# The end of an attention pipeline written as an order of its own, with two more buffers for expert weights

## The chip, the cores and the metric

The kernel runs on one core of a Trainium2 chip. The metric is the device time of one execution in microseconds (us). The kernel before took 780.9 us, the median of three runs (780.63 to 781.72).

## What is computed

Three stages follow each other. Attention has 4 x 8 heads of 576 tokens and 64 features, and keeps of each row the 32 largest scores. A soft mixture of experts (8 experts with 4 slots each) works on its output, and an MLP with a piecewise quadratic activation on that.

```python
scores = scale * np.matmul(q, k.transpose(0, 1, 3, 2))
kth = np.partition(scores, -32, axis=-1)[..., -32:-31]
scores = np.where(scores >= kth, scores, -1e9)
attn = softmax(scores)                    # over the keys
x = (attn @ v), heads side by side        # 2304 x 512
logits = x @ phi                          # 2304 x 32
d = softmax(logits, axis=0)               # over all tokens: what goes into a slot
slot_input = d.T @ x
slot_out[e] = np.maximum(slot_input[e] @ w1[e], 0) @ w2[e]
c = softmax(logits, axis=1)               # over the slots: back to the tokens
x = c @ slot_out
h = x @ w_in
g = where(h >= 1, h, where(h <= -1, 0, (h + 1) ** 2 / 4))
out = g @ w_out
```

## The kernel before

Attention works on 16 pairs of heads. A pair has five row blocks: blocks 0 to 3 have 128 query rows for each of two heads, block 4 the last 64 rows of both. Each block goes through some twenty steps, named by one letter, then row block and half: `S` scores on PE, `C` copies them to SBUF on ACT, `G` and `L` find the 24 largest on DVE, `M` masks what is among them (on POOL or DVE), `O` counts the mask on ACT, `X` makes the scores again on PE with the kept ones pushed far down by a product with the mask, `Y` takes the next eight by MAX8, `K` and `B` (POOL) make thresholds, `P` (ACT) and `U` (POOL) push down what is below them, `E` takes the exponential on ACT, `T` turns the row on PE into `pt_ps`, `Q` and `R` copy the turned row on ACT, `A` multiplies it with v on PE, `H` takes the result from PSUM on ACT. Blocks 3 and 4 of every pair go "by product": in place of `O` and `X`, a product on POOL (`V`, L418, tile `w`) takes the 24 largest out, and `M` is on DVE and counts as it masks.

`ORDER` is a list of these steps with a lag of 0 to 4 pairs. The loop at the end of the attention runs over frames; in frame f a step with lag k works on pair f - k. This is the order in which PE, ACT, DVE and POOL get their instructions (`manual_schedule`), and each takes them in that order. The last frames are the same list with the steps left out that have no pair any more. What follows the loop, `moe_last` (L671), was not in such an order: a planner placed its instructions.

In the last pair, blocks 3 and 4 take a shortcut (`last_pair`, L777): the exponential of the raw row (`ex`, L789) and the mask by threshold in one step on DVE (L791) in place of `P`, `U`, `E`. Its bias `nm` is made by POOL just before. Each row block of the last pair divides by its sum (`H`, L528), is turned once more (`xT_ps`) and copied to `xT`. `pt_ps` is one buffer of one PSUM bank.

`moe_last` then makes the logits of the last four pairs (`moe_ps`, L683) in three pieces of 256, 256 and 64 tokens; of each piece it takes the maximum, the exponential, turns it, multiplies it with x (`weigh`, L662) and adds it to `acc`. When `acc` is complete it is turned (`si_ps`) and copied to `siT`, which the first product of the experts (`ex_in`, L952) reads.

Expert weights are 64 tiles of 512 KB; the list `worder` says in which order SP loads them. `wload` takes the next free slot from `wfree`: tiles of their own first, then buffers of the attention that are used no more. Buffers of q and k, `ssb`, and four half-slot pairs (`xu` with `v_sb`, two of three `mb`, four `ptb`) come free in the drain, the four last ones after the loop (L823). After 36 tiles come two of w_out, then memory of the attention's pools.

Of the kernel before, what the change touches and what calls it, by code (L numbers as in the profile page):

```python
# [7 lines left out]
ET = mybir.EngineType  # L8
# [66 lines left out]
'''.split()  # L75
GA = 3
# [4 lines left out]
def kernel_body(tc, qT, kT, vP, phi, w1, w2, w_in, w_out, out, fast, flag):  # L81
# [35 lines left out]
    worder[36:36] = [(4, 0, f) for f in range(SOON)]  # L117
# [77 lines left out]
    n_x = sum(width) - n_v  # L195
    cnt_all = p_moe.tile([P, NPAIR * n_x], F32, name="cnt_all")
    less_all = p_moe.tile([P, NPAIR * n_v], F32, name="less_all")
    kn_all = p_moe.tile([P, NPAIR * n_v, 2], F32, name="kn_all")
# [82 lines left out]

    def at(u, j):
        of_v = u[1] in BY_V
        before = sum(width[r] for r in range(u[1]) if (r in BY_V) == of_v)
        return u[0] * (n_v if of_v else n_x) + before + j
# [84 lines left out]
    def op_m(u, j):  # L370
# [6 lines left out]
        if u[1] in BY_V:  # L377
# [42 lines left out]
    def op_y(u, j):  # L420
        if not fast:
            return
        if u[1] in BY_V:
# [34 lines left out]

    def op_t(u, j):
# [51 lines left out]
    def op_h(u):  # L511
# [9 lines left out]
        if r == 0:  # L521
            x_of[pi] = (p_xh.tile([P, 9, D], F32, name="xh", tag="xh"), p_xT.tile([P, S], F32, name="xT", tag="xT"))
        xh = x_of[pi][0]
        rd = p_small.tile([P, 2], F32, name="rd", tag="rd")
        nc.vector.tensor_scalar_add(rd[:, :n], av[:, :n, D], 1e-9)
        nc.vector.reciprocal(rd[:, :n], rd[:, :n])
        for j in range(n):
            nc.scalar.activation(xh[:, 2 * r + j, :], av[:, j, :D], AF.Copy, scale=rd[:, j:j + 1])  # L528
        emit_xT(pi, [r])
# [20 lines left out]
    def xT_flip(pi, rows):  # L550
        xh = x_of[pi][0]
        ps = ps_m.tile([P, NR, P], F32, name="xT_ps", tag="m_ps")
# [34 lines left out]
    def moe_quarters(b):  # L587
# [38 lines left out]
        nm = p_moe.tile([P, 1], F32, name="nmn", tag="nmn", bufs=3)  # L626
# [39 lines left out]
    def join_quarters():  # L666
        ps = ps_m.tile([P, P], F32, name="rq_ps", tag="m_ps")
        nc.tensor.matmul(ps[:, :1], same.rearrange("p r s -> p (r s)"), run_q, start=True, stop=True)
        nc.vector.tensor_copy(run_s, ps[:, :1])

    def moe_last(b, pieces, pool):  # L671
        def bank():
            nbank[0] += 1
            return pool.tile([P, 512], F32, name="moe_ps", tag=("s_ps", "x_ps", "pt_ps")[nbank[0] % 3], bufs=1)

        xs = [x_of[b * NHP + hp] for hp in range(NHP)]
        c0, c1 = pieces[0][0], pieces[-1][1]
        main = [r for r in range(NR) if c0 <= r * P < c1]
        mid = c1 == S
        for a, z in pieces:  # L680
            ps = bank()
            for c in range(NHP):
                nc.tensor.matmul(ps[:, :z - a], phi_sb[:, c].rearrange("p g s -> p (g s)"), xs[c][1][:, a:z],  # L683
                                 start=(c == 0), stop=(c == NHP - 1))
            yield
            nc.scalar.copy(lT[:, a:z], ps[:, :z - a])
            yield
        own = slice(b * NSLOT, (b + 1) * NSLOT)
        nc.vector.tensor_copy(lall[own, c0:c1], lT[own, c0:c1])
        mb = p_moe.tile([P, 1], F32, name="mb", tag="mb", bufs=3)  # L690
        nm = p_moe.tile([P, 1], F32, name="nmn", tag="nmn", bufs=3)
        nc.vector.reduce_max(mb, lT[:, c0:c1], axis=AX.X)
        nc.vector.scalar_tensor_tensor(nm, mb, -1.0, nrun[0], op0=ALU.mult, op1=ALU.min)
        before, nrun[0] = nrun[0], nm
        yield
        sb = p_moe.tile([P, 1], F32, name="sb", tag="sb", bufs=3)
# [655 lines left out]
```

## Time and profile before

| | |
|---|---|
| median of three runs | 780.9 us |
| the profiled execution, its own time | 781.92 us |
| its span, first to last instruction | 780.1 us |
| PE, DVE, ACT, POOL busy | 747.5, 649.7, 613.8, 491.5 us |
| granted TensorE clock, mean | 0.99 of full speed |
| read and written in HBM | 71.25 MB, 8.91 MB |

A busy PE means that matmuls are in flight; they overlap, and their ends are modelled. PEld is the loading of weights into the PE. The chain of work that ended last lies 55% on PE and 29% on DVE.

### The profile page before, as it was taken

The page shows a single profiled execution, that of the slowest core. Times are in us where ns is not written, and L with a number is a line of the kernel's source. Part 1 is how long each engine was busy: PE and PEld are TensorE (multiplying, and loading weights), DVE is VectorE, ACT ScalarE, POOL GpSimd, SP SyncE. Part 2 cuts the span into 40 slices and gives each one's busy share as a digit, 9 for nine tenths or more (in the row PEclk, how much of TensorE's full clock was granted, in tenths as well). Part 3 has the DMA queues.
Part 4 walks back from the last instruction along what each step waited for, and adds up shares of the span by engine and source line. Part 5 has one row for each costly group of instructions (what it writes and reads, how often), then busy time and mean ns, then how long its engine had stood idle before and what let it go on. Part 6 is the DMA issues. An engine that isn't in the chain of part 4 may idle for free.

```text
span 780.1 us, 15940 instructions
## 1 busy us (share of the span) xinstructions
PE 747.5 (96%) x5023; PEld 547.0 (70%) x5023; DVE 649.7 (83%) x2920; ACT 613.8 (79%) x1304; POOL 491.5 (63%) x532
## 2 busy tenths in 40 slices
PE   5899999999999999999999998898999999999996
PEld 2477777677777777777777777334577878888885
DVE  5999999999999999999999993162899977766662
ACT  3799999999999999999999995243688864555542
POOL 1899999999999999999999992020355500000000
PEclk9999999999999999999999998899999999999999
DMA  7414314304304312211220144999800020101001
GB/s 227 138 62 148 105 44 148 135 20 148 135 19 145 135 38 76 81 55 55 82 82 30 47 149 161 311 405 405 337 0 1 0 82 1 42 1 41 27 15 45
DMA packets 31726, 81.52 MB, mean 104 GB/s; under 512 B 5648, under 2 KB 6544, under 8 KB 31632
## 3 DMA queue, kind: packets, MB, share of 16 engines
q1 hardware_dynamic: 31344, 79.94, 28.8%
q8 instruction: 42, 0.69, 0.4%
q14 instruction: 52, 0.43, 0.2%
q10 hardware_dynamic: 288, 0.46, 0.2%
HBM read 71.25 MB, written 8.91 MB: 103 GB/s over the span
## 4 chain that ended last, share of the span: by engine, by line
PE 55%; DVE 29%; POOL 6%; ACT 4%; DMA 3%; issue 2%; ACTq 0%; POOLq 0%; DVEq 0%
PE o_ps L1158 19%; PE av_ps L506 8%; DVE cand L322 7%; PE s_ps L298 6%; DVE top L428 6%; PE pt_ps L465 5%; DVE cand L327 3%; DVE ghl L1142 3%; PE x_ps L298 3%; DVE top L329 2%; POOL ssb L454 2%; DVE mb L378 2%; PE h L952 2%; POOL mb L381 2%; PE h_ps L1110 2%
## 5 line engine op out<-in xcount | busy, mean ns | idle before, releaser
L1158 PE MATMUL o_ps<-whl,ghl 128*128 128x512 f32 x864 | 217.2, 395 | 1.2 <-DVE ghl L1124 0.5
L1158 PEld LDWEIGHTS o_ps<-whl,ghl 128*128 128x128 f32 x864 | 160.2, 188 | 38.2 <-DVE whl L1104 2.5
L454 POOL TENSOR_TENSOR ssb<-ssb,pen 128x576 f32<-128x576 f32 x141 | 180.5, 1285 | 2.5
L322 DVE MAX8 cand<-ssb 128x8 f32<-128x82 f32 (+1 forms) x1008 | 163.8, 235 | 5.8 <-ACT ssb L313 5.8
L506 PE MATMUL av_ps<-v_sb,ptb 128*128 128x65 f32 (+1 forms) x1280 | 144.4, 263 | 0.0
L506 PEld LDWEIGHTS av_ps<-v_sb,ptb 128*128 128x128 f32 (+1 forms) x1280 | 138.6, 183 | 5.8 <-issue 5.8
L381 POOL TENSOR_SCALAR mb<-ssb,top 128x576 bf16<-128x576 f32 x64 | 110.3, 1724 | 0.9 <-DVE top L329 0.9
L1113 ACT ACTIVATE rg<-h_ps,half 128x384 f32<-128x384 f32 (+1 forms) x98 | 56.1, 572 | 68.7 <-PE h_ps L1110 68.5
L298 PE MATMUL s_ps<-kt,qt 64*128 64x288 f32 x512 | 101.2, 473 | 8.7 <-ACT ssb L313 4.4
L313 ACT COPY ssb<-s_ps 128x576 f32<-128x576 f32 x144 | 95.7, 664 | 12.6 <-PE s_ps L298 10.4
L465 PE MATMUL pt_ps<-ident,ssb 128*128 128x128 f32 x640 | 100.3, 279 | 2.6 <-ACT ptb L481 2.4
L465 PEld LDWEIGHTS pt_ps<-ident,ssb 128*128 128x128 f32 x640 | 72.0, 146 | 30.4 <-ACT ptb L481 6.9
L1130 DVE SCALAR_TENSOR_TENSOR rg<-h_ps,rg 128x384 f32<-128x384 f32 x95 | 52.7, 555 | 36.3 <-ACT rg L1114 36.3
L481 ACT COPY ptb<-pt_ps 128x512 f32<-128x512 f32 x128 | 77.9, 608 | 3.9 <-PE pt_ps L465 3.9
L1093 POOL TENSOR_SCALAR tr_l<-tr_l 128x512 f32<-128x512 f32 x16 | 24.1, 1506 | 86.9 <-DVE tr_l L1092 60.9
L457 ACT ACTIVATE ssb<-ssb,kn 128x576 f32<-128x576 f32 x96 | 78.2, 814 | 0.7 <-POOL ssb L454 0.6
L451 ACT ACTIVATE pen<-ssb,kn 128x576 bf16<-128x576 f32 x96 | 75.2, 807 | 1.4 <-POOL kn L447 0.6
L428 DVE MAX8 top<-x_ps 128x8 f32<-128x584 f32 x96 | 72.7, 758 | 1.9 <-PE x_ps L412 1.6
L329 DVE MAX8 top<-cand 128x8 f32<-128x56 f32 x432 | 72.8, 205 | 0.1
L1142 DVE TENSOR_TENSOR ghl<-rg,ghl 128x384 fp32r<-128x384 f32 x95 | 67.7, 713 | 6.1 <-PE h_ps L1110 0.5
L298 PEld LDWEIGHTS s_ps<-kt,qt 64*128 64x128 f32 x512 | 40.3, 192 | 35.1 <-ACT ssb L313 11.3
L418 POOL TENSOR_TENSOR w<-ssb,mb 128x576 f32<-128x576 f32 x48 | 61.6, 1283 | 0.4 <-DVE mb L378 0.4
(234 smaller groups left out, 1296.8 us busy)
## 6 DMA issues: line engine op xcount, KB each, us to landing
w<-in_moe_w_dram SPq DMA_DIRECT2D x52, 512.0 KB, 6.9
x<-in_moe_w_in_dram SPq DMA_DIRECT2D x16, 512.0 KB, 3.8
w<-in_moe_w_out_dram SPq DMA_DIRECT2D x16, 512.0 KB, 10.1
w<-in_moe_w_dram SPq DMA_DIRECT2D x24, 256.0 KB, 5.0
kt<-in_k_dram SPq DMA_DIRECT2D x15, 360.0 KB, 4.4
v_sb<-in_v_dram SPq DMA_DIRECT2D x16, 325.0 KB, 7.0
qt<-in_q_dram SPq DMA_DIRECT2D x15, 320.0 KB, 5.3
out_dram<-o_sb SPq DMA_DIRECT2D x17, 256.0 KB, 2.2
```

Of the source, the lines that this page charges most:

```text
L298: nc.tensor.matmul(o, q[us], k[us, c:c + o.shape[-1]], start=True, stop=True, tile_position=(j * D, 0), skip_group_check=True)
L313: nc.scalar.copy(ssb[:, 0] if u[1] == NR else ssb[:, :, hf], st.pop((u, hf))[:, :, :HS])
L322: nc.vector.max(st[u]["cand"][:, j, 8 * g:8 * g + 8], row(u, j)[:, S * g // NSEG:S * (g + 1) // NSEG])
L329: nc.vector.max(t8, cand)
L381: nc.gpsimd.tensor_scalar(kept(u, j), row(u, j), t_u, None, op0=ALU.is_ge)
L428: nc.vector.max(st[u]["top"][:, j, TOPU:], src)
L454: nc.gpsimd.tensor_tensor(row(u, j), row(u, j), st.pop((u, "pen", j)), op=ALU.subtract)
L457: nc.scalar.activation(row(u, j), row(u, j), AF.Exp, bias=st[u]["kn"][:, j, 0:1], scale=0.125)
L465: nc.tensor.transpose(pt[:, c, :], pr[:, c0:c0 + P], ident)
L506: nc.tensor.matmul(o, pj[:, c, sl], v_sb[:, 4 * jj + c, :], start=False, stop=(c == NR - 1), skip_group_check=True)
L1142: nc.vector.tensor_tensor(gl, g, gh.bitcast(F32), op=ALU.subtract)
L1158: nc.tensor.matmul(pos[t][n], a[:, sl], w, start=(f == 0 and k == 0), stop=(f == NF - 1 and k == 2))
```

## The change

The loop over frames stops after frame 14. Frames 15 and on are replaced by `TAIL`, a list of 352 steps, each with its pair, in an order of its own for the four engines. The steps of `moe_last` are in that list too, cut up: `na`, `nb` (logits of the first three pairs, then of the last), `nc` copy, `nd` maximum, `nl` keep, `ne`, `nf` exponentials, `nt` turn, `ng` copy, `nw` weigh, `nx`, `ny` sums, for pieces 0 to 2; then `jp`, `jd`, `sp` and `sa`. Each piece has one bank of the former `x_ps`.

- The last pair's turns (`T`) alternate between the two banks of the former `s_ps`; its x is turned into `pt_ps` (`fl`), copied by a step of its own (`xc`), and its division is a step of its own (`rd`).
- `nm` is a step of its own: `nm3`, `nm4`.
- Row block 2 of the last pair goes by product too (`LAST_V`), with `V20`, `V21` on POOL; its `O` and `X` go.
- Slots for weights are given back at the step that ends their use (`freed`), and there are two more: both buffers of `w`, and the third `mb` with the second `v_sb`. Two w_out tiles come after 38 tiles instead of 36.

```diff
+FRAMES = 15
+TAIL = '''
+Y01.14 m09.11 C30.14 z4.14 O11.14 K10.14 T30.13 Q30.13 S31.14 U31.13 B0.14 L2.14 X10.14 K11.14
...
+P20.15 M30.15 T10.15 T11.15 rd0.15 H0.15 R1.15 lY.13 Q10.15 G40.15 lE.13 P31.15 lN.14 M31.15 lX.14
...
+U21.15 E21.15 T31.15 T21.15 R3.15 A30.15 Q31.15 nm4.15 V40.15 R2.15 K40.15 P40.15 Q21.15 Y40.15
+U40.15 A31.15 B4.15 A20.15 A21.15 rd3.15 rd2.15 T40.15 B3.15 H3.15 xc1.15 xc0.15 H2.15 T41.15 Q40.15
+Q41.15 R4.15 nb0.15 nc0.15 nd0.15 nl0.15 fl3.15 fl2.15 A40.15 xc2.15 A41.15 rd4.15 na1.15 ne0.15
+xc3.15 H4.15 nb1.15 fl4.15 nt0.15 na2.15 nc1.15 xc4.15 nd1.15 nb2.15 nf0.15 jp.15 ng0.15 nc2.15
+nd2.15 nw0.15 ne1.15 ne2.15 jd.15 ny0.15 nt1.15 nl2.15 nt2.15 nf2.15 nl1.15 ng1.15 nx0.15 nf1.15
+ng2.15 ny1.15 nw1.15 nw2.15 ny2.15 nx1.15 nx2.15 sp.15 sa.15
+'''.split()
+LAST_V = (2,)
-    worder[36:36] = [(4, 0, f) for f in range(SOON)]
+    worder[38:38] = [(4, 0, f) for f in range(SOON)]
+    def by_v(u):
+        return u[1] in BY_V or (u[0] == NPAIR - 1 and u[1] in LAST_V)
     def op_t(u, j):
-        pt = st[u, "pt", j] = ps_s.tile([P, NR, P], F32, name="pt_ps", tag="pt_ps", bufs=1)
+        if u[0] == NPAIR - 1:
+            if "t" not in last_ps:
+                last_ps["t"] = ps_s.tile([P, 2, NR, P], F32, name="lt_ps", tag="s_ps", bufs=1)
+                last_ps["n"] = 0
+            pt = st[u, "pt", j] = last_ps["t"][:, last_ps["n"] % 2]
+            last_ps["n"] += 1
...
+    frees = [[names(lastp - 1, "S", "X"), [qk_slot]], [tail_s | tail_x, [ssb_slot] * (NSSB - 5) + [qk_slot]]]
+    frees += [[{f"T{r}1.{lastp}"}, [ssb_slot]] for r in range(NR + 1)]
+    frees += [[{f"A{NR}1.{lastp - 1}", f"lN.{lastp - 1}"}, [xu_slot]], [tail_y, [w2_slot]]]
+    frees += [[tail_u | tail_x, [mb_slot]], [tail_u | tail_x | set(tail_a), [mv_slot]]]
+    ends = set(tail_a)
+    def freed(tok):
+        for left, slots in frees:
+            if tok in left:
+                left.discard(tok)
+                if not left:
+                    wfree.extend(slots)
+                    wload(99)
+        if tok in ends:
+            ends.discard(tok)
+            if len(ends) in (2, 0):
+                wfree.append(ptb_slot)
+                wload(99)
...
-        for frame in range(first, NPAIR + last + 1):
+        for frame in range(first, FRAMES):
...
-    wfree.extend(half_slots)
-    wload(99)
-    join_quarters()
-    gens = [moe_last(B - 1, [(lo, hi)], ps_s) for lo, hi in ((0, 2 * P), (2 * P, NR * P), (NR * P, S))]
+    with tc.manual_schedule(engines={ET.PE, ET.Activation, ET.DVE, ET.Pool}):
+        for tok in TAIL:
+            emit_tail(tok)
```

## Rows read from the trace of the kernel before

**Rows 1.** The page's slices of the span, busy share in tenths.

```profile
DVE  5999999999999999999999993162899977766662
POOL 1899999999999999999999992020355500000000
```

**Rows 2.** Windows: stretch, us, PE PEld DVE ACT POOL busy (count), clock, DMA.

```profile
392.30:421.00 28.70, 28.70 (x218) 21.37 (x216) 28.05 (x158) 28.50 (x67) 28.21 (x32) 1.00 0.20 68
421.00:450.00 29.00, 29.00 (x261) 22.04 (x260) 28.96 (x157) 27.63 (x60) 28.35 (x32) 1.00 0.13 41
450.00:478.50 28.50, 26.94 (x184) 21.84 (x184) 20.54 (x96) 23.89 (x54) 22.10 (x28) 0.88 0.43 139
478.50:497.55 19.05, 15.44 (x156) 12.08 (x155) 6.03 (x25) 8.52 (x32) 0.00 (x0) 0.94 0.78 248
421.00:497.55 76.55, 71.38 (x597) 55.95 (x595) 55.53 (x277) 60.04 (x144) 50.45 (x59) 0.94 0.40 129
486.20:497.55 11.35, 8.56 (x103) 5.93 (x102) 4.14 (x19) 4.54 (x20) 0.00 (x0) 0.91 0.88 277
```

**Rows 3.** Groups by line, 421:497.55: xcount | busy us, mean ns | idle before.

```profile
L381 POOL TENSOR_SCALAR mb<-ssb,top 128x576 bf16<-128x576 f32 x7 | 12.1, 1724 | 0.0
L481 ACT COPY ptb<-pt_ps 128x512 f32<-128x512 f32 x18 | 10.8, 602 | 2.0 <-PE pt_ps L465 2.0
L418 POOL TENSOR_TENSOR w<-ssb,mb 128x576 f32<-128x576 f32 x6 | 7.7, 1282 | 0.0
L391 ACT ACTIVATE ones<-mb 128x576 bf16<-128x576 bf16 x7 | 5.1, 729 | 0.0
L378 DVE TENSOR_SCALAR_CACHE_REDUCE mb<-ssb,top 128x576 bf16<-128x576 f32 x6 | 4.8, 795 | 0.0
L391 ACT ACTIVATION_READ_ACCUMULATOR ones<-mb 128x1 f32 x7 | 1.7, 245 | 0.0
```

**Rows 4.** Timeline: start us, us, engine, line, operation, out<-in, count, [idle before].

```profile
473.33 0.76 DVE L428 MAX8 top<-w 128x8 f32<-128x584 f32 x1
474.18 0.19 POOL L447 TENSOR_TENSOR kn_all<-top,factor 128x2 f32<-128x2 f32 x1 [2.06 <-DVE top L428]
474.34 0.23 POOL L787 TENSOR_SCALAR nm<-top 128x1 f32<-128x1 f32 x1
...
478.26 0.79 ACT L789 ACTIVATE ex<-ssb,nm 128x576 f32<-128x576 f32 x1
...
479.08 0.82 DVE L791 SCALAR_TENSOR_TENSOR ssb<-ssb,top,ex 128x576 f32<-128x576 f32 x1 [0.73 <-ACT ex L789]
...
486.20 0.48 PEld L465 LDWEIGHTS pt_ps<-ident,ssb 128*128 128x128 f32 x4
...
488.23 0.70 PE L683 MATMUL moe_ps<-xT,phi_sb 128*128 128x256 f32 x2 [0.36 <-ACT xT L568]
...
497.55 1.08 PE L952 MATMUL h<-w,siT 128*32 128x512 f32 x4 [0.35 <-ACT siT L837]
```

**Rows 5.** Windows, columns as in rows 2; DMA share and GB/s are last.

```profile
480.00:490.00 10.00, 8.63 (x73) 6.93 (x72) 1.95 (x9) 4.72 (x16) 0.00 (x0) 1.00 0.68 219
...
520.00:530.00 10.00, 9.64 (x79) 4.39 (x75) 6.69 (x14) 4.66 (x12) 1.99 (x2) 1.00 1.04 397
```

**Rows 6.** Waits of SP, 449 to 500: us in total, times, longest.

```profile
SPq L167 <- PE rem_ps L471: 12.8, 3, 7.1
```

**Rows 7.** Timeline of the experts' stage, PE, columns as in rows 4.

```profile
512.79 3.64 PE L952 MATMUL h<-w,siT 128*32 128x512 f32 x32
...
532.71 2.77 PE L975 MATMUL so<-w,h1T 128*32 128x512 f32 x22
535.65 1.90 PE L975 MATMUL so<-w,h1T 128*32 128x512 f32 x10 [0.16 <-DMA w<-in_moe_w_dram]
```

**Rows 8.** Windows at the lower clock, columns as in rows 2.

```profile
471.60:478.40 6.80, 6.69 (x28) 5.75 (x27) 3.64 (x11) 4.65 (x11) 0.82 (x4) 0.50 0.26 101
...
495.50:502.20 6.70, 5.78 (x41) 1.75 (x45) 0.50 (x2) 0.48 (x3) 0.00 (x0) 0.50 1.01 400
```

More of the change, by code (lines that the diff above doesn't have):

```diff
@@ L195, in kernel_body @@
     n_x = sum(width) - n_v
+    all_v = NPAIR * n_v + sum(width[r] for r in LAST_V)
     cnt_all = p_moe.tile([P, NPAIR * n_x], F32, name="cnt_all")
[L197 to L198 removed]
+    less_all = p_moe.tile([P, all_v], F32, name="less_all")
+    kn_all = p_moe.tile([P, all_v, 2], F32, name="kn_all")
     if fast:
@@ L280, in kernel_body @@
     xu_of = {}
+    def by_v(u):
+        return u[1] in BY_V or (u[0] == NPAIR - 1 and u[1] in LAST_V)
     def at(u, j):
+        if u[1] not in BY_V and by_v(u):
+            return NPAIR * n_v + sum(width[r] for r in LAST_V if r < u[1]) + j
         of_v = u[1] in BY_V
@@ L664, in weigh, with join @@
                                  stop=(n >= len(main) - 1), tile_position=(0, hp * NSLOT), skip_group_check=True)
[L666 to L677, printed above, removed]
+    def join(k):
+        if k == "p":
+            last_ps["j"] = ps_m.tile([P, P], F32, name="rq_ps", tag="m_ps")
+            nc.tensor.matmul(last_ps["j"][:, :1], same.rearrange("p r s -> p (r s)"), run_q, start=True, stop=True)
+        else:
+            nc.vector.tensor_copy(run_s, last_ps["j"][:, :1])
@@ new lines, in kernel_body, with slots_in, last_mix @@
+    siT = cpool.tile([P, NHP, NSLOT], F32, name="siT")
+    def slots_in(k):
+        if k == "p":
+            last_ps["s"] = ps_m.tile([P, P], F32, name="si_ps", tag="m_ps")
+            nc.tensor.transpose(last_ps["s"], acc, ident)
+        else:
+            nc.scalar.copy(siT.rearrange("p c s -> p (c s)"), last_ps["s"])
+    pieces = ((0, 2 * P), (2 * P, NR * P), (NR * P, S))
+    sums = {}
+    def last_mix(k, n):
+        xs = [x_of[(B - 1) * NHP + hp] for hp in range(NHP)]
+        c0, c1 = pieces[n]
@@ L678, in moe_last @@
         main = [r for r in range(NR) if c0 <= r * P < c1]
         mid = c1 == S
[L680 to L696, printed above, removed]
-        nc.scalar.activation(eT[:, c0:c1], lT[:, c0:c1], AF.Exp, bias=nm, scale=1.0, accum_out=sb)
@@ L698, in moe_last @@
-        al = p_moe.tile([P, 1], F32, name="al", tag="al", bufs=3)
-        nc.scalar.activation(al, before, AF.Exp, bias=nm, scale=-1.0)
-        yield
-        ps = bank()[:, :(NR + 1) * NSLOT].rearrange("p (r s) -> p r s", s=NSLOT)
-        eye = ident[:NSLOT, :NSLOT]
-        for r in main:
-            nc.tensor.transpose(ps[:, r, :], eT[:NSLOT, r * P:(r + 1) * P], eye)
-        if mid:
-            for jj in range(2):
-                sl = slice(jj * REM, (jj + 1) * REM)
-                flip(ps[sl, NR, :], eT[:NSLOT, NR * P:], eye, jj)
@@ L860, in kernel_body @@
     wload(NB)
+    ring = [x for x in ring if x not in (w2_slot, mv_slot)]
     held = [x for x in slots_a + cv_slots if x in ring][-9:]
```

182 lines of the change are left out of this document (125 added, 57 removed).

## The prediction

> **What bounds the kernel now.** I read the page first: the engines' shares and the slices. DVE and POOL show nines for the first 23 of 40 slices; then both fall, POOL to 0 [rows 1]. That hollow is the seam between attention and the experts, so I cut the span into stages [rows 2]. In a repeating frame (392.3 to 421.0 us, 28.7 us) ACT is busy 28.50, POOL 28.21, DVE 28.05: three engines full at once, and an order written by hand holds each at 98% or more. The two frames in which the last block leaves the pipeline are another matter. From 450.0 to 478.5 ACT has 23.89 of 28.5, POOL 22.10, DVE 20.54; from 478.5 to 497.55 DVE has 6.03 of 19.05, ACT 8.52, POOL nothing. At 497.55 the first expert product starts [rows 4]. So no engine bounds the drain: order does.
>
> The timeline of the drain shows how [rows 4]. The last row block's MAX8 on the product (`Y40`) begins at 473.33, but its mask step on DVE (`U40`) begins only at 479.08, since the exponential that it needs starts at 478.26. That exponential needs `nm`, which stands on POOL behind the block's `kn_all`, and that one waited 2.06 us for the MAX8. Behind it four turns of `pt_ps` follow each other through a single buffer. The last one starts at 486.20, and from there to the expert product runs a chain of 11.35 us.
>
> The weights are the second limit. DMA moves 219 GB/s from 480 to 490 and 397 from 520 to 530 [rows 5]; SP's longest waits before a load of weights are on PE, which has to release tiles (12.8 us in three times on `rem_ps`) [rows 6]. The last half tile of the second expert matrix arrives when PE is there: 32 products take 3.64 us where weights lie ready, and the last 32 take from 532.71 to 537.55, 4.84 us, with a wait on the DMA [rows 7]. So the experts run about 1.2 us behind their weights, and no more.
>
> **Part by part.** The trace up to 421 repeats frames 0 to 14, which the change leaves as they are: nothing there. All terms are for 421.0 to 497.55.
>
> Row block 2 of the last pair goes by product. POOL loses two masks of 1.724 us and gains two products of 1.282: 0.88 less. ACT loses two counting copies of 0.729 + 0.245: 1.95 less. DVE gains two masks of 0.795: 1.59 more [rows 3]. PE loses nine score and mask products, about 1 us at the frames' pace worked out below. Remaining work: ACT 60.04 - 1.95 = 58.1, POOL 50.45 - 0.88 = 49.6, DVE 55.53 + 1.59 = 57.1 us [rows 2]. DVE's two extra masks stand ahead of the products that POOL makes; that is covered as long as DVE, idle for 21.0 us of this stretch, is not late there, and costs 1.6 us if it is.
>
> The order. Three paths lead to the expert product.
> POOL: its work at the frames' 98% ends at 421 + 49.6/0.98 = 471.6. Then the MAX8 0.76, the mask step 0.82, one turn of about 0.6 and hops of some 0.3 (the exponential now stands ahead of them): last turn at 474.1, and with today's chain of 11.35 us 485.4.
> ACT: 4.54 of its us lie inside the last 11.35 us [rows 2]; the other 53.6 at 98% take 54.7, the chain then starts at 475.7, and ends at 487.0.
> PE: 597 matmuls less 9, at the full frame's 261 in 29.0 us, 0.111 each, are 65 us, or 486.0. This is above its need, as other engines paced that frame.
> The latest is 487.0. What is late next is the chain itself: turn, copy, product with v, scale, turn, logits, maximum, exponential, turn, weighing, sum, turn, copy; the change shortens no link of it. Within it ACT's copies for rows 2 and 3 and for the earlier pieces now crowd in, where today some lie ahead of it. Bounds: a chain with nothing beside it, 485.4; with ACT's fill of the old drain (23.89/28.5 = 0.84) over the last frame alone, some 4 us more than 487.0, 491. I take 488.0, nearer to the good end: the full frames show what a written order can hold. That is 9.6 us.
>
> Two banks for the turns. With one buffer the copies wait 2.0 us for turns in all [rows 3]; that is inside the 9.6 and not added. The Trainium skill's PSUM — Partial Sum Buffer page (PSUM bank collisions) has a rule that speaks against the other half, three pieces with logits, turned exponentials and weighed sum in one bank each: two engines must not touch one bank and quadrant at once, so neighbours in a bank must be serialised. Here the three uses follow each other by data in any case; by the rule nothing would be added to the sum, except where a piece's copy runs under its own next product, and no trace here shows that.
>
> Logits in pieces. The logits of the first three heads run ahead today too: after the last head's copy two instructions of `moe_ps` are left, 0.70 us [rows 4]. The change writes down what is there; 0, bounds 0.7 either way.
>
> Moved loads and two more buffers. SP issues in program order, so each load waits behind the earlier tokens' releases. Released earlier and two tiles more, 1 MB, at 397 GB/s 2.6 us of loading, lie ahead of the experts. Queued behind: the two w_out tiles, now after tile 38, and the tiles that reuse the attention's memory. The first are read by the MLP's preparation only and the others late in the experts' stage, so I cost that at 0; it is 2.6 us if the second matrix's last tile comes to stand behind them. Gain: the 1.2 us wait at the end, bounds 0 and 1.2; I take 0.5, since the experts also start 9.6 us earlier and the loads must keep up.
>
> Clock. The granted clock is at its lower level, 1.2 GHz, from 471.6 to 478.4 and from 495.5 to 502.2 [rows 8]. In each case PE had thin work before it. The second stretch covers the first 4.7 us of the expert products, at half speed: 2.4 us, if it goes. With a chain as thin as today's I leave it in place: 0, bounds 0 and 2.4 gained, or 3.4 lost (a further stretch of 6.8 us at half speed).
>
> Other edits (checks two columns wider, one more small buffer, `siT` allocated early): no change in a row's length, 0; at most 0.2 us either way.
>
> Sum: 9.6 + 0.5 = 10.1 us. Span 780.1 - 10.1 = 770.0. The profiled execution took 781.9, 1.8 more than its span, and is 1.0 above the median 780.9 of three; the median is thus 0.8 above that span, and I forecast 770.8.
>
> **Rivals.**
> PE is the bound. Its row reads 26.94 of 28.50 and 15.44 of 19.05, so only 5.2 us of the drain are free: 780.9 - 5.2 = 775.7. Against it: weight loads fill 21.84 and 12.08 of these, and the same engine passes 261 matmuls per 29.0 us where 184 and 156 stand here. The Trainium skill's Perfetto Trace Analysis (Identifying the Most-Contended Engine) says that matmul busy time is a poor measure, as matmuls are pipelined, and weight-load time a better one; by it PE has 0.23 to 0.37 of these stages free, which the counts bear out. Chance 0.15.
>
> The weights take over. If SP's queue is held by a late release, the second expert matrix ends at its old time of 535.6 and the earlier drain is waited out on PE: only the 1.2 us and the tail of the copy remain, 779.7, or about 776 if half is recovered. For: from 520 the DMA is full at 397 GB/s, and the experts' start moves. Against: at 219 GB/s before 490 almost half of that is free, and SP waits on PE, not on the DMA. Chance 0.09, of which 0.04 near 780.
>
> Slower: the written order blocks. Each engine takes its queue in written order, so one late step holds all behind it on four engines; the new list replaces also the frame from 421 to 450, today full at 27.63 to 28.96 of 29.0. If ACT's 53.6 us run at a fill f, the expert product starts at 421 + 53.6/f + 11.35. It is past 497.55 + 1.6 at f below 0.80; the old drain had ACT at 0.84, DVE at 0.72. At 0.76 it is 502.9, 5.4 us later: 786. Against: the frames before keep 0.98 by such a list. Chance 0.10.
>
> The new list leaves as many holes as today's, elsewhere: 780.9. Chance 0.03, in "same" with the weights' 0.01.
>
> **How the numbers follow.** Forecast 0.63 (766 to 773.5), PE 0.15, weights 0.09, slower 0.10, nothing 0.03. Faster by over 0.2%, about what a measurement of this kernel can tell from no change, is 0.63 + 0.15 + 0.08 = 0.86; same 0.04; slower 0.10. The range reaches up past PE's 775.7 to 777.5, and down to 765.5: 485.4 for 488.0, the whole 1.2, and part of the 2.4 of the clock.
>
> **What would show it.** Right: frames to 421 alike; no `nm` behind a waiting `kn_all`; ACT, DVE and POOL above 0.9 until about 470; the last POOL product at 470 to 473; the first expert product at 486 to 490; DMA above 350 GB/s before it; the last 32 expert products in 3.7 to 4.4 us. Wrong: expert products waiting on DMA by several us; ACT below 0.85 between 421 and 475; a chain after the last turn longer than 13 us; or the MLP stage, unchanged in work, longer by over 1 us through its buffers' new order.

## The result and the profile after

The changed kernel takes 772.4 us, the median of five runs (771.83 to 773.18); the kernel before took 780.9 beside it (779.75 to 782.91, five runs). The ratio is 0.9887, with a 95% interval of 0.9875 to 0.99. The profiled execution took 771.83 us, with a span of 770.0; it is the fastest of the five. That is the span that was forecast, to the tenth, and as the places of the gain below show, part of this is luck. The median lies 1.6 us above the forecast of 770.8, within the range. The forecast put the median 0.8 us above the span, as it was before, and here it is 2.4 above.

The first view is the page's slices of the kernel after, the lines that answer to [rows 1]:

```profile
DVE  5999999999999999999999996173899967776662
POOL 2899999999999999999999995030455400000000
```

Behind the nines the slice is fuller, 6 for 3 on DVE and 5 for 2 on POOL. The windows by stage of the kernel after (us, then busy time of PE, PEld, DVE, ACT, POOL with counts, clock, DMA share, GB/s) cut the drain at the two last turns (475.62) and at the first expert product (489.73), and end with the experts' stage:

```profile
421.00:475.62 54.62, 54.04 (x434) 43.64 (x426) 50.82 (x252) 50.79 (x112) 50.07 (x59) 1.00 0.34 109
475.62:489.73 14.11, 10.73 (x114) 8.17 (x113) 4.92 (x23) 6.17 (x28) 0.00 (x0) 0.86 1.04 375
489.73:531.83 42.10, 40.03 (x320) 15.06 (x321) 15.69 (x32) 13.07 (x27) 5.84 (x4) 0.96 0.99 381
```

Up to the last turns DVE, ACT and POOL are each full to 0.92 or 0.93, at a full clock. Before, the same engines fell from about 28 of 29 us to 21 to 24 of 28.5, and then to 6.0, 8.5 and 0 of 19 [rows 2]. The low stretch of the clock from 471.6 to 478.4 [rows 8] is not there in the kernel after. DMA moves 375 GB/s from the last turns to the first expert product. The experts' stage before ran from 497.55 to 541.64:

```profile
497.55:541.64 44.09, 41.92 (x321) 15.36 (x321) 15.61 (x32) 12.81 (x27) 5.82 (x4) 0.95 1.02 394
```

Not all of what lies between the two traces is due to the change. Both kernels go through frames 0 to 14 with the same steps. One row of POOL near the end of frame 14 can serve as a common mark, first in the kernel before, then in the kernel after:

```profile
419.27 1.16 POOL L250 TENSOR_TENSOR tr<-tr,sg 128x512 f32<-128x512 f32 x1
```

```profile
418.06 1.16 POOL L280 TENSOR_TENSOR tr<-tr,sg 128x512 f32<-128x512 f32 x1
```

The kernel after is 1.2 us ahead at this mark already. In the traces of all kernels of this document the mark lies between 418.06 and 419.27, so this is scatter between executions; what makes it, no run shows. From the mark to the first expert product it is 78.3 us before (497.55) and 71.7 after (489.73). So the 10.1 us of span have four places: 1.2 ahead of the mark, 6.6 in the drain, 2.0 in the experts' stage (44.09 to 42.10), 0.3 in the 238 us behind it. The last three make 8.9 us, and the medians differ by 8.5.

The timeline of the drain after (start us, us, engine, line, operation, out<-in, count, idle before and its releaser) answers to [rows 4]:

```profile
469.67 0.73 POOL L592 TENSOR_SCALAR nm<-top 128x1 f32<-128x1 f32 x1
...
472.36 0.79 ACT L851 ACTIVATE ex<-ssb,nm 128x576 f32<-128x576 f32 x1
...
472.85 0.77 DVE L463 MAX8 top<-w 128x8 f32<-128x584 f32 x1 [1.81 <-POOL w L472]
...
473.73 0.82 DVE L853 SCALAR_TENSOR_TENSOR ssb<-ssb,top,ex 128x576 f32<-128x576 f32 x1
...
475.62 1.04 PE L509 MATMUL lt_ps<-ident,ssb 128*128 128x128 f32 x8
...
482.50 0.37 ACT L760 COPY lT<-lm_ps 128x256 f32<-128x256 f32 x1 [2.62 <-PE lm_ps L757]
...
482.77 0.22 ACT L628 COPY xT<-lx_ps 128x64 f32<-128x64 f32 x1
...
483.04 0.43 PE L757 MATMUL lm_ps<-xT,phi_sb 128*128 128x64 f32 x2 [0.58 <-ACT xT L628]
...
486.41 1.08 PE L721 MATMUL lm_ps<-xh,et 128*32 128x128 f32 x16 [1.08 <-ACT er L791]
...
488.05 0.73 DVE L798 SCALAR_TENSOR_TENSOR acc<-acc,al,lm_ps 128x128 f32<-128x128 f32 x2 [1.33 <-PE lm_ps L721]
...
489.73 11.97 PE L1049 MATMUL h<-w,siT 128*32 128x512 f32 x96 [0.35 <-ACT siT L739]
```

Three things are to be seen. The last MAX8 comes 54.8 us behind the mark (472.85), 0.7 later than before (473.33) [rows 4]: up to there nothing is gained. From it to the last turn it is now 3.2 us (the row of eight holds the last two turns; the second starts at 476.06), where it was 13.0 (its matmuls start at 486.31): here lies the gain of the drain, 9.8 us. From the last turn to the expert product it is 13.7 us, where it was 11.2 (11.35 from the loading of its weights, as the prediction counts): 2.4 us are lost again. The waits in the rows at 482.50, 486.41 and 488.05 all stand on `lm_ps` (at 486.41 PE waits for ACT's copy `er`, which reads `lm_ps`).

The 9.8 us need not all be the order's. Before, the first 5 us of that stretch ran at the lower clock, and in the whole low stretch PE was busy for 6.69 us [rows 8]; at the full clock half of that would do, so by this estimate up to 3.3 us could be the clock's. The lower clock is also in the traces of e6_before_nm_early and e7_old_order, in which the old order stands, and in none of the others from 421 to 485.9. No run parts the two.

### The profile page after: what moved, and what is told of

It reads as the page before. It is cut to its first block, busy times and chain, and to the rows that moved or that the text cites. A ratio compares the mean times of both kernels' runs of the same rounds, so it can differ in the third digit from the quotient of the medians.

```text
span 770.0 us, 15917 instructions
## 1 busy us (share of the span) xinstructions
PE 736.8 (96%) x5014; PEld 542.5 (70%) x5014; DVE 651.0 (85%) x2924; ACT 612.2 (80%) x1300; POOL 491.7 (64%) x532
## 4 chain that ended last, share of the span: by engine, by line
PE 58%; DVE 24%; POOL 7%; DMA 6%; issue 2%; ACT 1%; SPq 1%; DVEq 0%; POOLq 0%; ACTq 0%
PE o_ps L1255 19%; PE av_ps L550 10%; PE s_ps L333 6%; PE pt_ps L509 6%; DVE cand L357 5%; DVE top L463 4%; DMA w<-in_moe_w_dram 3%; PE x_ps L333 3%; DVE ghl L1239 3%; POOL ssb L489 3%; DVE cand L362 2%; DVE top L364 2%; POOL mb L416 2%; PE av_ps L548 2%; PE h_ps L1207 2%
## 5 line engine op out<-in xcount | busy, mean ns | idle before, releaser
L1210 ACT ACTIVATE rg<-h_ps,half 128x384 f32<-128x384 f32 (+1 forms) x98 | 56.0, 572 | 68.3 <-PE h_ps L1207 68.3
L333 PE MATMUL s_ps<-kt,qt 64*128 64x288 f32 x512 | 99.5, 466 | 8.7 <-ACT ssb L348 4.4
L416 POOL TENSOR_SCALAR mb<-ssb,top 128x576 bf16<-128x576 f32 x62 | 106.9, 1724 | 0.9 <-DVE top L364 0.9
L509 PE MATMUL pt_ps<-ident,ssb 128*128 128x128 f32 x600 | 93.8, 279 | 1.9 <-ACT ptb L525 1.8
L509 PEld LDWEIGHTS pt_ps<-ident,ssb 128*128 128x128 f32 x600 | 67.0, 146 | 29.5 <-ACT rs L533 6.8
L492 ACT ACTIVATE ssb<-ssb,kn 128x576 f32<-128x576 f32 x94 | 76.6, 816 | 0.1
L525 ACT COPY ptb<-pt_ps 128x512 f32<-128x512 f32 x120 | 73.0, 608 | 2.3 <-PE pt_ps L509 2.1
L463 DVE MAX8 top<-x_ps 128x8 f32<-128x584 f32 x94 | 71.1, 758 | 3.2 <-PE x_ps L447 2.8
L453 POOL TENSOR_TENSOR w<-ssb,mb 128x576 f32<-128x576 f32 x50 | 64.6, 1293 | 1.2 <-DVE mb L413 1.2
```

Of the source, the lines that this page charges most:

```text
L333: nc.tensor.matmul(o, q[us], k[us, c:c + o.shape[-1]], start=True, stop=True, tile_position=(j * D, 0), skip_group_check=True)
L416: nc.gpsimd.tensor_scalar(kept(u, j), row(u, j), t_u, None, op0=ALU.is_ge)
L463: nc.vector.max(st[u]["top"][:, j, TOPU:], src)
L492: nc.scalar.activation(row(u, j), row(u, j), AF.Exp, bias=st[u]["kn"][:, j, 0:1], scale=0.125)
L509: nc.tensor.transpose(pt[:, c, :], pr[:, c0:c0 + P], ident)
```

## The experiments

The runs were compared with the kernel before on their own chip, where it took 781.95 to 782.74 us in the median; so ratios are read side by side, and stages in us within the traces. As the mark scatters by up to 1.2 us, two traces are compared by the time from the mark, which the table gives for the last turn and the first expert product beside the time in the trace. The stages behind the experts keep their length in all of them, 237.9 to 238.6 us. The intervals of e3_no_extra_buffers, e5_one_bank and e9_no_product_checks_late overlap that of the kernel after, and that of e8_busy_pe overlaps that of e2_all_own_tiles; there the rows of the traces carry the reading.

| kernel | median us | ratio, 95% interval | mark | last turn (from the mark) | first expert product (from the mark) | last 32 expert products, us |
|---|---|---|---|---|---|---|
| before | 780.9 | 1 | 419.27 | 486.31 (67.0) | 497.55 (78.3) | 4.84 |
| after | 772.4 | 0.9887, 0.9875 to 0.99 | 418.06 | 476.06 (58.0) | 489.73 (71.7) | 3.64 |
| e1_own_tiles | 768.95 | 0.9838, 0.9808 to 0.9869 | 418.11 | 476.12 (58.0) | 486.69 (68.6) | 3.64 |
| e2_all_own_tiles | 769.21 | 0.9845, 0.9814 to 0.9876 | 418.53 | 476.27 (57.7) | 486.84 (68.3) | 3.64 |
| e3_no_extra_buffers | 774.92 | 0.9916, 0.9885 to 0.9946 | 418.39 | 476.38 (58.0) | 490.05 (71.7) | 6.15 |
| e4_no_product | 776.13 | 0.9927, 0.9904 to 0.9951 | 418.70 | 479.44 (60.7) | 493.10 (74.4) | 3.64 |
| e5_one_bank | 776.87 | 0.9914, 0.9889 to 0.994 | 419.15 | 480.62 (61.5) | 494.35 (75.2) | 3.64 |
| e6_before_nm_early | 782.24 | 0.9988, 0.9972 to 1.0004 | 418.20 | 485.47 (67.3) | 496.70 (78.5) | 5.42 |
| e7_old_order | 792.8 | 1.0109, 1.0073 to 1.0144 | 419.26 | 493.45 (74.2) | 511.12 (91.9) | 3.65 |
| e8_busy_pe | 773.5 | 0.9877, 0.9853 to 0.9901 | 418.72 | 476.46 (57.7) | 492.62 (73.9) | 3.64 |
| e9_no_product_checks_late | 775.32 | 0.991, 0.9892 to 0.9928 | 418.87 | 479.61 (60.7) | 493.57 (74.7) | 3.64 |
| e10_checks_late | 768.44 | 0.9828, 0.9809 to 0.9846 | 418.12 | 475.86 (57.7) | 486.43 (68.3) | 3.64 |
| e11_short_fill | 768.24 | 0.9825, 0.9806 to 0.9844 | 418.37 | 476.11 (57.7) | 487.20 (68.8) | 3.74 |

### One tile for three banks: e1_own_tiles and e2_all_own_tiles

In the kernel after, the copy of piece 1 (`nc1`, 482.50) waits 2.62 us for PE's logits of piece 2, which lie in another bank of the same tile; its own logits were there at 480.98. The first experiment gives each piece a tile of its own; to make room for these, `x_ps` gets a pool of its own that ends before them. Nothing else changes:

```diff
...
-    last_ps["b"] = ps_s.tile([P, 3, 512], F32, name="lm_ps", tag="x_ps", bufs=1)
-bank = last_ps["b"][:, n]
+    st_x.close()
+    ps_l = att.enter_context(tc.tile_pool(name="ps_l", bufs=1, space=PSUM))
+    last_ps["b"] = [ps_l.tile([P, 512], F32, name=f"lm{i}_ps", tag=f"lm{i}", bufs=1) for i in range(3)]
+bank = last_ps["b"][n]
```

> The changed kernel, but each of the three logit pieces has a PSUM tile of its own instead of a third of one tile lm_ps (same three banks, same order of steps). Theory A: the chain from the last turn to the experts took 13.6 us and more instead of the 11.35 of the sum, because steps of one piece wait for steps of another that stand ahead of them in the list and write or read the same tile, though another bank (copy of piece 1 at 482.50 waits for the product of piece 2; second weighing at 486.41 for the copy of piece 2). With own tiles the expert product starts 2 to 3 us before today's 489.7, and the time falls from 772.4 to about 769.5 to 770.5. Theory B: these waits are data and queue order of the work itself, so at most 0.5 us falls away: 772.

The timeline of e1_own_tiles, the same steps as at 482.50, 482.77, 486.41, 488.05 and 489.73 above:

```profile
481.09 0.37 ACT L764 COPY lT<-lm_ps 128x256 f32<-128x256 f32 x1 [1.14 <-PE lm_ps L761]
...
481.52 0.21 ACT L630 COPY xT<-lx_ps 128x64 f32<-128x64 f32 x1
...
484.42 0.65 PE L723 MATMUL lm_ps<-xh,et 128*32 128x128 f32 x16
...
485.13 0.35 DVE L802 SCALAR_TENSOR_TENSOR acc<-acc,al,lm_ps 128x128 f32<-128x128 f32 x1
...
486.69 1.86 PE L1053 MATMUL h<-w,siT 128*32 128x512 f32 x8 [0.35 <-ACT siT L741]
```

The copy goes 1.4 us earlier, right behind its own logits, and the waits of the weighing and of the sum are gone. The last turn stays where it was, and from it to the expert product it is now 10.6 us, 3.1 less than in the kernel after and shorter than the 11.2 of the kernel before. The interval of the ratio does not overlap that of the kernel after. So these waits came from the one tile and not from the data. Some 0.7 of the 3.1 us are the clock's: in the kernel after the last weighings and the turn of `acc` fall into the low stretch that begins at 486, in e1_own_tiles they are over when it begins, at about 486.8, and take 0.7 us less of PE (16 products of the weighing 0.65 us for 1.08). Whether the waits also bring the clock down earlier is not shown. By the Trainium skill's PSUM — Partial Sum Buffer page (PSUM bank collisions) guarding is wanted by bank and quadrant; by that rule the three banks needed no wait between them, and the trace agrees once each is a tile.

The second experiment does the same to the two banks of the turns (`lt_ps`), on top of the first:

```diff
...
-pt = st[u, "pt", j] = last_ps["t"][:, last_ps["n"] % 2]
+pt = st[u, "pt", j] = last_ps["t"][last_ps["n"] % 2]
```

> As the kernel with own tiles for the pieces, and the two banks of the last pair's turns are two tiles too. Theory A: a copy of a turned row then no longer waits for the turn after it (the copy of row block 4's first half waits 0.6 us for its second half): 0.5 to 1.5 us more than with own pieces alone, about 769. Theory B: the turns are paced by ACT, which has no time to copy earlier: no more than 0.3 us.

From the mark the last turn and the expert product come 0.3 us earlier than in e1_own_tiles, and the median is no lower: the turns lose at most that by their one tile. There Theory B held.

### The two extra buffers: e3_no_extra_buffers

```diff
-worder[38:38] = [(4, 0, f) for f in range(SOON)]
+worder[36:36] = [(4, 0, f) for f in range(SOON)]
-frees += [[{f"A{NR}1.{lastp - 1}", f"lN.{lastp - 1}"}, [xu_slot]], [tail_y, [w2_slot]]]
-frees += [[tail_u | tail_x, [mb_slot]], [tail_u | tail_x | set(tail_a), [mv_slot]]]
+frees += [[{f"A{NR}1.{lastp - 1}", f"lN.{lastp - 1}"}, [xu_slot]]]
+frees += [[tail_u | tail_x, [mb_slot]]]
```

> The changed kernel without the two added load buffers: two w_out tiles come after 36 expert tiles again. Order, turns, pieces unchanged. Theory A (the sum): the added buffers are worth what PE no longer waits at the end of the second expert matrix, 0.5 to 1.2 us, as now the last 32 products take 3.64 us and took 4.84: time 773 to 773.6, with the wait back in these products. Theory B: the loads are what lets the earlier start count at all, and without the two buffers the experts wait for 2 tiles of 1.3 us each: 2.5 us or more, 775.

The drain keeps its time (71.7 us from the mark). What comes back is the wait of [rows 7], and it is longer now. The last 32 expert products in the timeline of e3_no_extra_buffers:

```profile
524.18 2.77 PE L1072 MATMUL so<-w,h1T 128*32 128x512 f32 x20
...
527.16 1.05 PE L1072 MATMUL so<-w,h1T 128*32 128x512 f32 x2 [0.20 <-DMA w<-in_moe_w_dram]
...
528.42 1.91 PE L1072 MATMUL so<-w,h1T 128*32 128x512 f32 x10 [0.22 <-DMA w<-in_moe_w_dram]
```

They take 6.15 us, and with the buffers they take what PE needs:

```profile
524.04 3.64 PE L1072 MATMUL so<-w,h1T 128*32 128x512 f32 x32
```

The buffers are thus worth 2.5 us of PE's time. The span is 3.0 longer (773.0 for 770.0), of which 0.3 lie ahead of the mark. The windows from 475.62 to 490.00 of the kernel after and of e3_no_extra_buffers show where they work:

```profile
475.62:490.00 14.38, 11.00 (x118) 8.38 (x121) 4.92 (x23) 6.17 (x28) 0.00 (x0) 0.86 1.03 371
```

```profile
475.62:490.00 14.38, 11.05 (x117) 8.50 (x116) 5.22 (x25) 6.53 (x30) 0.00 (x0) 0.86 0.88 304
```

At 371 GB/s for 304 over 14.38 us, 0.96 MB more arrives before the experts: about the two tiles.

### Row block 2 by product: e4_no_product and e9_no_product_checks_late

```diff
-LAST_V = (2,)
+LAST_V = ()
-T31.14 P01.15 R3.14 P00.15 M20.15 U01.15 A21.14 E40.14 Q31.14 U00.15 M21.15 V20.15 X11.15 S40.15
-H2.14 T40.14 A30.14 E01.15 E00.15 Y10.15 Q40.14 Y11.15 G30.15 B1.15 C40.15 V21.15 A31.14 P10.15
...
+M21.15 O20.15 X11.15 S40.15 H2.14 T40.14 A30.14 E01.15 E00.15 Y10.15 Q40.14 Y11.15 G30.15 B1.15
+C40.15 O21.15 X20.15 A31.14 P10.15 H3.14 T41.14 T00.15 T01.15 U10.15 P11.15 R4.14 Q41.14 A40.14
+K20.15 Q00.15 K21.15 X21.15 A41.14 R0.15 G31.15 Q01.15 E10.15 L3.15 nm3.15 Y20.15 H4.14 P30.15
```

> The changed kernel with row block 2 of the last pair as in the pairs before: masks on POOL, counting copies on ACT and score and mask products on PE in place of the products on POOL. Theory A: ACT is the engine that the drain's fill hangs on, so its 1.95 us come back nearly whole: expert product 1 to 2 us later, time 773.4 to 774.4. Theory B: none of the four engines is full before the last turn (ACT 0.93), the order has room: within 0.5 us of 772.4.

From the mark the last turn and the expert product come 2.7 us later (493.10 for 489.73 in the traces, of which 0.6 lie ahead of the mark). In the waits of DVE in e4_no_product (line waited for: us, times, longest) the longest is that of the check `cnt_all`, which stands early in the order and now needs the counts that ACT makes in `O`:

```profile
DVE cnt_all L936 <- ACT rs L534: 3.0, 1, 3.0
```

That could have been the whole cost, and a fault of the place of the check rather than of the work. The second run puts the checks behind the last block:

```diff
...
-xc2.15 A41.15 rd4.15 na1.15 ne0.15
+xc2.15 A41.15 rd4.15 ck.15 na1.15 ne0.15
...
+        elif name == "ck":
+            check()
...
```

> The kernel without the product for row block 2 (last pair), with one more edit: the final checks on counts and thresholds, which the planner put into DVE's queue from 462.7 on, come after the last division instead. Theory A: of the 3.4 us that taking the product back cost, some 2 to 2.5 are DVE held for 3.0 us by the first check, which waits for the last count, and POOL and the turns behind it; the work itself is worth 1 us. Expected expert product at 490.5 to 491.5 (493.1 with the checks early, 489.7 with the product), time 773.4 to 774.4. Theory B: the product is worth the 3.4 us itself: 492.5 or later, 775.5 or more.

The cost stays: the last turn is where it was in e4_no_product, and the expert product comes 3.0 us later than in the kernel after. The waits of DVE in e9_no_product_checks_late show the next cause in the place of the one removed:

```profile
DVE top L464 <- PE x_ps L448: 6.0, 3, 3.9
```

MAX8 waits for PE's second scores, which wait for the mask and its count; in the kernel after, DVE waits for `x_ps` for 0.9 us in all. `O` and `X` put two engines between mask and MAX8; the product on POOL is one step. So in this order the product is worth about 3 us (2.7 and 3.0), more than the 1.95 us that ACT is spared, and the trace puts the wait on the longer chain. Where `O` and `X` stand in the list had to be chosen; what the best list with them would lose is not shown.

### One bank for the last pair's turns: e5_one_bank

```diff
-pt = st[u, "pt", j] = last_ps["t"][:, last_ps["n"] % 2]
+pt = st[u, "pt", j] = last_ps["t"][:, 0]
```

So that the written order can run with one buffer, each turn of the last pair stands behind the copy of the turn before it.

> The changed kernel with one bank for the last pair's turns in place of two: a turn comes after the copy of the turn before it, as in the kernel before; everything else is in the same order. Theory A (the sum): with one buffer ACT's copies waited 2.0 us for turns; so the expert product starts 1 to 2 us later, 773.4 to 774.4. Theory B: a copy waits for the turn after its own anyhow, since both banks are one tile, and own tiles for the banks brought nothing; so one bank costs at most 0.5 us: 772 to 773.

The timeline of e5_one_bank:

```profile
472.80 0.59 ACT L526 COPY ptb<-lt_ps 128x512 f32<-128x512 f32 x1 [1.15 <-PE lt_ps L510]
...
476.48 0.27 ACT L534 COPY rs<-rem_ps 128x128 f32<-128x128 f32 x1 [1.48 <-PE rem_ps L516]
476.64 0.78 ACT L852 ACTIVATE ex<-ssb,nm 128x576 f32<-128x576 f32 x1
...
480.62 0.66 PE L510 MATMUL lt_ps<-ident,ssb 128*128 128x128 f32 x4 [0.88 <-ACT ptb L529]
```

The last turn waits for the copy of the one before it, and the exponential, which in the kernel after stood ahead of the last MAX8 (472.36), comes at 476.64, behind a copy that waits for its own turn. From the mark the expert product comes 3.5 us later. The idle time before the copies in the kernel before was 2.0 us [rows 3]: the visible wait was little more than half of what the second bank is worth here. The edit also moves turns in the order, so the 3.5 belongs to bank and order together.

### `nm` ahead of `kn_all` in the kernel before: e6_before_nm_early

```diff
+if pi == NPAIR - 1 and name in ("V30", "V40"):
...
+    nm = st[u]["nm"] = p_small.tile([P, 2], F32, name="nm", tag="nm", bufs=2)
+    nc.gpsimd.tensor_scalar(nm[:, :n], st[u]["top"][:, :n, 0], -0.125, None, op0=ALU.mult)
...
-                if j == 0:
-                    nm = st[u]["nm"] = p_small.tile([P, 2], F32, name="nm", tag="nm", bufs=2)
...
```

> The kernel before, with one edit: POOL makes the bias nm of the last pair's row blocks 3 and 4 ahead of their product, not behind kn_all. Theory A: the exponential of row block 4 started 3.9 us after nm could be had and the turn waited for it, so 1 to 2 us of the gain are in this alone: 779 to 780 where the kernel before has 780.9. Theory B: ACT's queue and PE's queue hold that exponential and the turns behind it as well, whatever nm does: within 0.5 us of 780.9.

The timeline of e6_before_nm_early:

```profile
469.46 0.22 POOL L770 TENSOR_SCALAR nm<-top 128x1 f32<-128x1 f32 x1
...
471.72 0.77 DVE L428 MAX8 top<-w 128x8 f32<-128x584 f32 x1 [0.17 <-POOL w L437]
...
476.91 0.82 DVE L792 SCALAR_TENSOR_TENSOR ssb<-ssb,top,ex 128x576 f32<-128x576 f32 x1 [1.43 <-ACT ex L790]
...
485.47 0.60 PE L465 MATMUL pt_ps<-ident,ssb 128*128 128x128 f32 x4
```

In the traces `nm` comes 4.9 us earlier, the mask step 2.2 and the last turn 0.8. But this execution is 1.1 us ahead at the mark (418.20 for 419.27): from there the mask step comes 1.1 us earlier, and the last turn and the expert product 0.2 later. The ratio's interval holds 1. Theory B held: the late `nm` did not bind. The rows of the prediction could have told: `nm` was done at 474.57, and the exponential began 3.7 us later [rows 4]. Behind the mask step the turns still stood in their old order behind one buffer.

### The new steps in the old order: e7_old_order

```diff
-Q40.13 X20.14 c0.15 c1.15 S00.15 E00.14 M30.14 K21.14 P10.14 T41.13 G40.14 H2.13 R4.13 U01.14 X21.14
...
+E00.14 Y11.14 M30.14 K20.14 T41.13 O21.14 U01.14 G40.14 B1.14 H3.13 R4.13 K21.14 S00.15 V30.14
...
-LAST_V = (2,)
+LAST_V = ()
```

From frame 15 on the steps stand in the order of the repeating list; `rd` stands before `fl`, `xc` behind each `H`, and the pieces' steps behind `xc1`, behind `xc3` and at the end.

> The changed kernel with the attention steps of the last frames in the order of the repeating list, the steps of its own (division, turn and copy of x) beside the step that they came from, the logit pieces behind them, and row block 2 of the last pair not by product, since that list has no room for it. Two banks, own steps, buffers as changed. Theory A: the interleaved order brings most of the gain: expert product at 495 or later, time 777 to 781. Theory B: cutting the work into steps, early release of loads and placing the pieces bring most, the order little: 774 to 776, no more than the kernel without the product (776.1).

All of the change but the order (and the product) is there, and the kernel is 1.1% slower than the one before. The timeline of e7_old_order:

```profile
473.33 0.76 DVE L464 MAX8 top<-w 128x8 f32<-128x584 f32 x1
...
475.22 3.55 PE L758 MATMUL lm_ps<-xT,phi_sb 128*128 128x256 f32 x8
...
490.14 3.52 PE L551 MATMUL av_ps<-v_sb,ptb 128*128 128x65 f32 x16
493.24 0.87 PEld L510 LDWEIGHTS lt_ps<-ident,ssb 128*128 128x128 f32 x4
```

and two of its windows:

```profile
482.00:499.00 17.00, 15.47 (x64) 13.13 (x64) 1.50 (x6) 3.77 (x11) 0.00 (x0) 0.50 0.43 145
502.00:516.00 14.00, 11.38 (x91) 6.25 (x95) 2.78 (x13) 2.71 (x14) 0.00 (x0) 0.52 0.91 320
```

The last MAX8 begins to the hundredth where it did before, 473.33, and the last turn 20 us behind it. Eight matmuls for logits, 3.55 us, now stand ahead of turns and hold them; and PE runs at the lower level of its clock for most of the 34 us from 482 on, where 16 products with v take 3.52 us for the 1.90 of the kernel after. It was worse than either theory said. The expert product comes 13.6 us later than in the kernel before, and much of that can be the clock: up to it PE was busy for some 24 us at the lower level, 16 more than in the kernel before, and half of that, an estimate, is 8 us. The other 5 or more are not, so the new steps and buffers bring no gain in this order, not even with the clock taken out. Where the new steps stand in the old list had to be chosen, and the product for row block 2 is missing too; what the best old order would give is not shown.

### Fill for PE ahead of the experts: e8_busy_pe, e10_checks_late, e11_short_fill

In the kernel after the clock still falls at 486, and its low stretch covers 3 us of the expert products. e8_busy_pe is e2_all_own_tiles with seven products of 512 columns in PE's gaps:

```diff
+elif name[:2] == "dm":
+    for _ in range(int(name[2])):
+        nc.tensor.matmul(last_ps["t"][0].rearrange("p a b -> p (a b)"), ident,
+                         phi_sb.rearrange("p c g s -> p (c g s)"), start=True, stop=True)
```

> The kernel with own tiles for pieces and turns, and seven products of 512 columns more on PE (0.43 us each at the full clock, result unused), in the gaps of the last chain: one before the last logits, two before and one after the second weighing, two before and one after the last turn. Theory A: thin work lets the clock fall there; the added products keep it at 2.4 GHz, the 96 expert products take 10.3 to 10.6 us in each run, not 12; time 767 to 768. Theory B: the clock does not depend on these gaps, or what is added stands in the way: 769 to 770.5.

The timeline of e8_busy_pe, two of the seven products and the first 96 of the experts:

```profile
485.61 1.98 PE L907 MATMUL lt_ps<-phi_sb,ident 128*128 128x512 f32 x4
...
492.62 10.51 PE L1057 MATMUL h<-w,siT 128*32 128x512 f32 x96
```

The clock stays up and the 96 products take 10.51 us for the 11.97 of the kernel after; but in e2_all_own_tiles, without the fill, they take 10.51 too. Each added product stands as two matmuls in the row (four for two), and costs nearly twice what was put in: from the mark the expert product comes 5.6 us later than in e2_all_own_tiles.

e10_checks_late is e2_all_own_tiles with the checks behind the last block (the edit of e9_no_product_checks_late); e11_short_fill adds six turns of 128 columns in the same gaps.

> The kernel with own tiles for pieces and turns, with the final checks after the last division instead of where the planner put them. Theory A: the checks stand between two divisions at 474.5 to 475.7, and ACT waits 1.7 us there for a division; without them the last turn comes 0.3 to 1 us earlier and the time is 0.3 to 1 us below the 769.2 of own tiles. Theory B: the divisions are not on the path, the last turn waits for PE's products: no difference over 0.3 us.

> As the one before, and six short turns of 128 columns (result unused) on PE in the gaps of the last chain: one before the last logits and before each of the two last weighings, two before and one after the last turn. The seven long products cost 5.8 us and took the low stretch away. Theory A: six short turns cost under 0.5 us; what PE is busy with there decides on the clock, so the low stretch goes or stays as in the runs without them by chance, and if it goes the 96 expert products take 10.5 us, not 12: 0 to 1.5 us below the kernel without them. Theory B: they stand in the way by their full length, 0.22 us each: 0.5 to 1.3 us slower.

The windows from 480 to 486 and from 486 to 490, first of e10_checks_late, then of e11_short_fill:

```profile
480.00:486.00 6.00, 5.13 (x73) 3.69 (x71) 3.61 (x18) 2.87 (x14) 0.00 (x0) 1.00 1.04 401
486.00:490.00 4.00, 3.64 (x21) 0.91 (x24) 0.00 (x0) 0.27 (x1) 0.00 (x0) 0.57 1.03 412
```

```profile
480.00:486.00 6.00, 5.76 (x77) 4.18 (x76) 3.52 (x18) 2.87 (x14) 0.00 (x0) 1.00 1.05 396
486.00:490.00 4.00, 3.60 (x32) 1.26 (x36) 0.35 (x1) 0.27 (x1) 0.00 (x0) 1.00 1.03 416
```

With the short turns the profiled run has no low stretch here, the expert product comes 0.5 us later from the mark, and the first 96 products take 10.51 us for 12.13. The medians are 768.24 and 768.44: no difference that could be measured. The profiled run of e2_all_own_tiles has no low stretch here either, without any fill; e10_checks_late, with the same order of PE's work, has one. So the stretch comes and goes by itself, and what the turns did to it stays open, as it does for the seven products of e8_busy_pe. The later checks change nothing: from the mark, last turn and expert product come when they do in e2_all_own_tiles. The versions with own tiles, at 0.9825 to 0.9845, lie together, and they are faster than both kernels.

## Why the prediction was right, step by step

The time and the likeliest case were right. Not all terms were: the drain gained 6.6 us of the 9.6 of its term, and the stages behind it gained 1.8 us more than theirs. That the span was met to the tenth is luck: the missing 3.0 us are filled by these 1.8 and by the 1.2 that lie ahead of the mark. By the medians 8.5 us were gained of the 10.1.

**The order, up to the last turn: right, and some 1.5 us too early.** ACT's path put the start of the last chain at 475.7 in the time of the kernel before, 56.4 us behind the mark; the last turn starts 58.0 behind it, 1.6 later, where 1.0 had been added for crowding in all. POOL's last product was put at 471.6, 52.3 behind the mark, and ends at 472.47, 54.4 behind it. ACT, DVE and POOL were to stay above 0.9 until about 470, and are at 0.92 or 0.93 in the mean of 421 to 475.62. But what was read as the cause, the late `nm`, was not one (e6_before_nm_early: nothing gained at the expert product). What the order took away are the 9.8 us between last MAX8 and last turn, perhaps with the help of a clock that no longer falls there; e7_old_order shows that the new steps without the order bring nothing in the place that they had there.

**The chain behind the last turn: the step that failed.** It was taken at 11.35 us with 1.0 us for crowding ("the change shortens no link of it"); it took 13.7. The prediction gave more than 13 us as a sign of error, and it was one: 3.1 of these us go when each of the three banks is a tile of its own (e1_own_tiles), some 2.4 of them as waits and 0.7 by the clock. The prediction looked at neighbours within a bank, and costed logits in pieces at 0; the waits ran between banks. Without them the chain takes 10.6 us, so the change does shorten it, by some 0.7, and from the mark to the expert product it is 68.6 us, where the forecast of 488.0 meant 68.7. So the drain's term of 9.6 would have been met (9.7), and the waits through one tile are what it lacked.

**The two buffers: sign right, size not.** 0.5 us was taken, bounds 0 and 1.2. The experts' stage got the whole 1.2 (4.84 to 3.64 us), the upper bound. Undone, they cost 2.5 (e3_no_extra_buffers): the experts start earlier, the same loads are late by more, and so the wait measured before was no bound on what a buffer is worth after.

**The clock: 0 taken, 0.9 gained at the experts.** The second low stretch stayed, as forecast. But it now begins at 486, 3.7 us ahead of the experts instead of about 2, and the first 96 products take 11.97 us for 12.83. It lies within the bounds. With the 1.2 of the buffers it makes the 2.0 us of the experts' stage, 1.5 more than the 0.5 of the sum; 0.3 more come in the stages behind. That the first low stretch might go was not considered; it went, and what it is worth inside the drain is open, 3.3 us at most by the estimate above.

**Row block 2 by product and the two banks: counted in the wrong unit.** Both were put inside the 9.6, the one as 1.95 us of ACT's work, the other as 2.0 us of waiting. Undone alone they cost about 3 and 3.5 us at the expert product. In an order in which each engine takes its steps as written, a step that comes late delays those behind it as well. These prices overlap with each other and with the order's, and do not add up to the gain.

**The rivals.** PE as the bound allowed the drain to lose 5.2 us at most; it lost 6.6, and 9.7 with own tiles. (PE's busy time there held the 6.69 us at the lower clock; with the 3.3 of the estimate above the bound would be 8.5, and the own tiles pass that too.) By the Trainium skill's Perfetto Trace Analysis page (Identifying the Most-Contended Engine) matmul busy time is a poor measure of how near PE is to its limit. The trace agrees, as matmuls were in flight for 26.94 of 28.50 us and the drain could still be shortened by more than what was free. The weights did not take over. Without the two buffers they would have taken 2.5 us back, but the kernel would still have been faster than the rival's 776 to 779.7 (e3_no_extra_buffers: 774.92, beside 781.95 for the kernel before). That a written order blocks is real: in e5_one_bank an exponential stands behind a waiting copy, and e7_old_order ends slower than before, by 1.1%, in part by its clock. In the list of the change ACT is full to 0.93 up to the last turns, where that rival needed less than 0.80.

## What to carry to other kernels

At a seam between two stages, read the time from the last result of one engine to the first use of it on the next: here that stretch held 13.0 us, and the engines' shares told only that something was loose. Before two traces are compared by the clock time of an event, set them to a common mark behind the part that is the same in both: here that part alone differed by 1.2 us, more than some of the effects looked for. Buffers that are used independently should be tiles of their own: here the waits followed the tile and not the bank (e1_own_tiles, 3.1 us), though the two banks of the turns lost at most 0.3 us by it (e2_all_own_tiles). An idle time in the trace of before is no upper bound on what a buffer or a shorter chain is worth in an order that runs tighter.

## What was not expected of the hardware

TensorE's granted clock fell to its lower level, 1.2 GHz, at 486 us in the kernel after although matmuls were in flight for 4.39 of the 6 us before; in e10_checks_late it fell after 5.13 of 6. In e2_all_own_tiles, with PE's work in the same order, it did not fall there. What decides is not shown. The windows of the kernel after:

```profile
480.00:486.00 6.00, 4.39 (x41) 3.15 (x39) 2.04 (x10) 2.55 (x13) 0.00 (x0) 0.99 1.04 393
486.00:490.00 4.00, 2.22 (x37) 1.59 (x41) 1.32 (x6) 0.61 (x3) 0.00 (x0) 0.50 1.00 328
```

The other surprise is the price of a float32 product of 512 columns: in e8_busy_pe it stands as two matmuls, and seven of them cost 5.6 us where 3.0 had been put.
